# First token block on plain f32 passes, W_out decoded between its products, row sums in two accumulators, and a fixed order at the start

## The chip, the cores and the metric

The kernel runs on one core of one Trainium2 chip. The metric is the device time in microseconds of one execution, as the median of several runs. TensorE is called PE, VectorE DVE, ScalarE ACT, GpSimd POOL; SP is the queue on SyncE that issues all transfers.

## The reference

Agent attention over four batches, and a feed-forward layer on what it gives. q, k and the agents are normal with a spread of 0.8, v with 0.1; the weights are float64.

```python
B, N, C = (4, 12480, 128)       # q, k, v: [4, 12480, 128]; agents: [4, 49, 128]
n_tokens, d_model, d_ff = (49920, 128, 2048)

def sm(a, b):
    s = scale * (a @ b.transpose(0, 2, 1))
    s = s - s.max(-1, keepdims=True)
    e = np.exp(s)
    return e / (e.sum(-1, keepdims=True) + 1e-09)
a2k = sm(agents, k)
agent_v = a2k @ v
q2a = sm(q, agents)
x = (q2a @ agent_v).reshape(B * S, D)
h = x @ w_in
g = h - np.tanh(h)
return (g @ w_out).astype(np.float32)
```

## The kernel before

**Two parts.** For each batch a first phase makes `avs`, the normalized agent_v turned to [128 channels, 49 agents] and written twice side by side, and multiplies it by W_in. The result, 98 rows of 2048 hidden units, is stored as a rounded part `awh` (the type that TensorE takes in one pass) and the rest `awl`. The main part then runs over 104 blocks of 480 tokens, 26 a batch. A block has eight steps `i`; a step handles two chunks of 128 hidden units:

- `m1` (L441, L442): four products, `awh` and `awl` with the block's transposed softmax weights `pT`, into the PSUM tile `h` (three buffers).
- `act`: y = tanh on ACT (L451), z = y squared on ACT (L453), g = h z on DVE (L455).
- `high` (L485): POOL rounds g to `gh`. `low` (L490): DVE takes the rest, `gl`. They run one step behind.
- `m2` (L502 to L504): per chunk three products, `wo_l` with gh, `wo_h` with gh, `wo_h` with gl, summed in a PSUM tile of the pool `misc` (two buffers). The last step of every even block is "plain": one f32 product a chunk with the unrounded copy `wo_f` (L500), and neither gh nor gl.

The softmax of q (`q_softmax`, two blocks at a time: L396, L406 to L421) and its transposes (`q_transpose`, L428, L433) run beside this, and so do the first phases of batches 1 to 3 (generators in `kq`, three started in each pair of blocks).

**The start.** Batch 0 has no block to hide behind. Its first phase reads K in 13 tiles of up to 1024 keys (`kt`), forms the scores (L212), copies them to `s` (ACT, L223) and takes maxima (DVE, L225). After the last tile the maxima are joined and spread as `mb` (L267). Then per tile of V: subtract (DVE, L276), exponential (ACT, L278), product with V (L292). The row sums are formed by adding all tiles of exponentials in `es` (DVE, L305), a reduction (L308) and three products with a column of ones (L316). `sums` adds the two halves of the PSUM tile, divides, transposes (L338) and writes `avs` (L340, L343). `project` makes awh and awl in five parts (L370, L373, L374), and takes the maximum of each part (L376) for a test that comes at the very end.

**The weights.** W_in and W_out come as raw 64-bit words in pieces of 512 columns (`raw`). `decode` turns a piece to f32: one operation on ACT (L128) and six on DVE (L129 to L134). For W_out, `load_w_out` then makes `wo_h` (ACT, L156), `wo_l` (DVE, L157) and from the last piece `wo_f` (ACT, L159). Two pieces of W_out are loaded among the K tiles and decoded during the V stage, two come behind the V tiles and are decoded behind `avs`.

**What sets the order.** Each engine runs its instructions in the order of the built program. A scheduler that simulates a timeline chooses it; `hold` adds the few edges that keep some decode work on DVE behind a named instruction, and `loads_first` keeps the early transfers in the order written.

Of the kernel before, what the change touches and what calls it, by code (L numbers as in the profile page):

```python
# [15 lines left out]
I64 = mybir.dt.int64  # L16
# [33 lines left out]
R0 = 6  # L50
# [6 lines left out]
NB = dict(y=2, z=2, g=4, gh=3, gl=2)  # L57
QL = 0
# [17 lines left out]
class Build:  # L76
# [19 lines left out]
    def constants(self):  # L96
# [7 lines left out]
        nc.vector.tensor_copy(self.identr, self.ident)  # L104
        self.ones = c.tile([128, 128], F32, tag="ones", name="ones")
# [8 lines left out]
        for vt in self.vb:  # L114
            nc.gpsimd.memset(vt[:, :, C : C + 1], 1.0)
# [3 lines left out]
    def decode(self, raw, dst):  # L119
# [8 lines left out]
        nc.scalar.activation(size, hi.bitcast(F32), AF.Abs)  # L128
        nc.vector.tensor_scalar(ta, hi, 3, 0x3FFFFFF8, ALU.logical_shift_left, ALU.bitwise_and)  # L129
        nc.vector.scalar_tensor_tensor(ta, hi, 0xC0000000, ta, ALU.bitwise_and, ALU.bitwise_or)  # L130
# [3 lines left out]
        nc.vector.scalar_tensor_tensor(dst, size, TINY, rem, ALU.is_ge, ALU.mult)  # L134
# [605 lines left out]
```

## Time and profile before

| what | value |
|---|---|
| median of 3 runs | 2185.13 us (2184.85 to 2185.13) |
| the profiled execution | 2180.92 us, its span 2179.1 us |
| busy in the span | PE 98%, DVE 93%, ACT 83%, POOL 64% |
| chain that ended last | PE 88%, DVE 6%, POOL 3%, waiting to issue 2% |
| batch 0's last K product | starts at 30.0 us |
| first and last product with V | 35.1 and 50.5 us |
| `avs` complete | 59.6 us |
| first tanh, first g of block 0 | 70.3 and 73.0 us |

The profiled execution is 4.2 us shorter than the median, 0.2%. Times inside it are us from the start of the span. A product of f32 operands appears as two records, one of the rounded type as one. A group's mean is the time of one instruction; followers on one engine overlap a little, so the distance between two starts can be shorter.

### The profile page before, as it was taken

The page shows a single profiled execution, that of the slowest core. Times are in us where ns is not written, and L with a number is a line of the kernel's source. Part 1 is how long each engine was busy: PE and PEld are TensorE (multiplying, and loading weights), DVE is VectorE, ACT ScalarE, POOL GpSimd, SP SyncE. Part 2 cuts the span into 40 slices and gives each one's busy share as a digit, 9 for nine tenths or more (in the row PEclk, how much of TensorE's full clock was granted, in tenths as well). Part 3 has the DMA queues.
Part 4 walks back from the last instruction along what each step waited for, and adds up shares of the span by engine and source line. Part 5 has one row for each costly group of instructions (what it writes and reads, how often), then busy time and mean ns, then how long its engine had stood idle before and what let it go on. Part 6 is the DMA issues. An engine that isn't in the chain of part 4 may idle for free.

```text
span 2179.1 us, 31204 instructions
## 1 busy us (share of the span) xinstructions
PE 2144.5 (98%) x11089; PEld 1799.3 (83%) x11089; DVE 2026.2 (93%) x2120; ACT 1813.1 (83%) x2179; POOL 1395.5 (64%) x933
## 2 busy tenths in 40 slices
PE   7899999999999999999999999999999999999998
PEld 7688878888888887888888888888888888888887
DVE  7898999999999999889999999998999999999998
ACT  4688888888888788888898878888889898989987
POOL 1356567666666556667666556667667677676766
PEclk9799999999999999999999999999999999999999
DMA  9211111110011111111101110121100101010000
GB/s 353 86 58 60 56 38 57 59 57 28 28 48 57 59 48 46 58 59 48 37 19 57 57 50 19 56 65 33 36 20 19 37 19 37 19 37 19 28 10 20
DMA packets 65906, 108.75 MB, mean 50 GB/s; under 512 B 4048, under 2 KB 44240, under 8 KB 65744
## 3 DMA queue, kind: packets, MB, share of 16 engines
q1 hardware_dynamic: 65744, 106.68, 15.2%
q8 instruction: 91, 1.49, 0.3%
q14 instruction: 71, 0.58, 0.1%
HBM read 81.10 MB, written 25.56 MB: 49 GB/s over the span
## 4 chain that ended last, share of the span: by engine, by line
PE 88%; DVE 6%; POOL 3%; issue 2%; ACT 0%; DMA 0%; POOLq 0%; SPq 0%; DVEq 0%; ACTq 0%
PE h L441 15%; PE h L442 15%; PE misc L504 15%; PE misc L502 14%; PE misc L503 14%; PE misc L500 4%; PE misc L396 4%; PE misc L238 3%; POOL gh L485 2%; DVE gl L490 2%; DVE g L455 2%; PE misc L292 2%; PE misc L428 1%; PE h L212 1%; PE misc L370 0%
## 5 line engine op out<-in xcount | busy, mean ns | idle before, releaser
L485 POOL TENSOR_SCALAR gh<-g 128x960 fp32r<-128x960 f32 x780 | 1207.3, 1549 | 665.0 <-DVE g L455 416.5
L490 DVE TENSOR_TENSOR gl<-g,gh 128x960 fp32r<-128x960 f32 x780 | 977.4, 1254 | 89.8 <-PE misc L504 55.7
L455 DVE TENSOR_TENSOR g<-h,z 128x960 f32<-128x960 f32 x832 | 950.5, 1146 | 30.5 <-ACT z L453 27.3
L451 ACT ACTIVATE y<-h 128x960 f32<-128x960 f32 x832 | 802.9, 970 | 186.2 <-PE h L442 182.1
L453 ACT ACTIVATE z<-y 128x960 f32<-128x960 f32 x832 | 832.4, 1007 | 24.3 <-DVE g L455 7.2
L441 PE MATMUL h<-pT,awh 98*128 98x480 f32 x1664 | 662.0, 398 | 1.9 <-DVE awl L374 1.4
L442 PE MATMUL h<-pT,awl 98*128 98x480 f32 x1664 | 631.7, 380 | 0.3 <-DVE awl L374 0.3
L504 PE MATMUL misc<-gl,wo_h 128*128 128x480 f32 x1560 | 607.6, 390 | 3.0 <-DVE gl L490 2.9
L502 PE MATMUL misc<-gh,wo_l 128*128 128x480 f32 x1560 | 601.8, 386 | 4.9 <-POOL gh L485 4.9
L503 PE MATMUL misc<-gh,wo_h 128*128 128x480 f32 x1560 | 593.9, 381 | 0.0
L441 PEld LDWEIGHTS h<-pT,awh 98*128 98x128 f32 x1664 | 313.5, 188 | 65.9 <-issue 13.2
L442 PEld LDWEIGHTS h<-pT,awl 98*128 98x128 f32 x1664 | 315.2, 189 | 57.5 <-issue 10.5
L502 PEld LDWEIGHTS misc<-gh,wo_l 128*128 128x128 f32 x1560 | 294.4, 189 | 59.9 <-POOL gh L485 15.7
L504 PEld LDWEIGHTS misc<-gl,wo_h 128*128 128x128 f32 x1560 | 292.6, 188 | 56.4 <-DVE gl L490 7.9
L503 PEld LDWEIGHTS misc<-gh,wo_h 128*128 128x128 f32 x1560 | 293.3, 188 | 47.1 <-issue 1.2
L409 POOL TENSOR_TENSOR qe<-qe,qm 120x392 f32<-120x392 f32 x52 | 74.2, 1426 | 63.7 <-ACT qe L407 63.7
L396 PEld LDWEIGHTS misc<-ag,qt 128*120 128x120 f32 x832 | 96.3, 186 | 4.0 <-issue 0.3
L617 ACT ACTIVATE o<-misc 128x480 f32<-128x480 f32 x104 | 58.7, 564 | 48.7 <-PE misc L500 33.6
L396 PE MATMUL misc<-ag,qt 128*120 128x49 f32 x832 | 93.6, 265 | 0.0
L500 PE MATMUL misc<-g,wo_f 128*128 128x480 f32 x208 | 92.9, 569 | 0.0
L421 POOL TENSOR_TENSOR pp<-qe,pp 120x392 fp32r<-120x392 f32 x52 | 69.4, 1335 | 36.6 <-ACT pp L419 36.4
L238 PEld LDWEIGHTS misc<-ag,kt 128*128 128x128 f32 x588 | 72.1, 191 | 2.5
(92 smaller groups left out, 864.0 us busy)
## 6 DMA issues: line engine op xcount, KB each, us to landing
qt<-qT SPq DMA_DIRECT2D x52, 480.0 KB, 3.4
outT<-o SPq DMA_DIRECT2D x52, 480.0 KB, 2.6
kt<-kT SPq DMA_DIRECT2D x48, 512.0 KB, 3.6
v<-v SPq DMA_DIRECT2D x36, 512.0 KB, 4.1
vt<-v SPq DMA_DIRECT2D x12, 512.0 KB, 9.4
raw<-w_in SPq DMA_DIRECT2D x4, 512.0 KB, 9.1
raw<-w_out SPq DMA_DIRECT2D x4, 512.0 KB, 8.9
kt<-kT SPq DMA_DIRECT2D x4, 128.0 KB, 2.1
```

What stands on the lines that cost most here:

```text
L396: nc.tensor.matmul(ps[:TT, t * A : (t + 1) * A], qt[:, t * TT : (t + 1) * TT], self.ag[:, b, :], start=True, stop=True)
L441: nc.tensor.matmul(h[:, c, :BLK], aw[0][:A2, sl], pT[:A2], start=True, stop=False)
L442: nc.tensor.matmul(h[:, c, :BLK], aw[1][:A2, sl], pT[:A2], start=False, stop=True)
L451: nc.scalar.activation(y, h[:, :, :BLK], AF.Tanh, scale=TSC)
L453: nc.scalar.activation(z, y.rearrange("p c n -> p (c n)"), AF.Square)
L455: nc.vector.tensor_tensor(self.pair(g), h[:, :, :BLK], self.pair(z), ALU.mult)
L485: self.nc.gpsimd.tensor_scalar(gh, g, 1.0, 0.0, ALU.mult, ALU.add)
L490: self.nc.vector.tensor_tensor(gl, g, gh.bitcast(F32), ALU.subtract)
L500: nc.tensor.matmul(acc[:, :BLK], self.wo_f[:, c, :], gh[:, x], start=first, stop=last)
L502: nc.tensor.matmul(acc[:, :BLK], self.wo_l[:, f, :], gh[:, x], start=first, stop=False)
L503: nc.tensor.matmul(acc[:, :BLK], self.wo_h[:, f, :], gh[:, x], start=False, stop=False)
L504: nc.tensor.matmul(acc[:, :BLK], self.wo_h[:, f, :], gl[:, x], start=False, stop=last)
```

## The change

**Block 0 in f32.** Every step of block 0 is plain: its products take W_out in f32 (`wf`, 2048 columns, kept in the buffer that batch 1's `awh` will take) and the unrounded g. So block 0 needs no gh, no gl and neither half of W_out. **Decode between its products.** `decode` becomes a generator; its steps are taken by hand, three at a time, before and between the steps of block 0, in work tiles that gh and gl do not use yet. All four pieces of W_out load behind V, into the four buffers that batch 1's V takes later (the ones in their last column are set after). `split_w_out` makes wo_h on ACT and wo_l now on POOL, one piece at each of four steps of block 1. **Row sums.** Two accumulators `es` take turns and are joined; a product with a matrix of ones spreads the sums to all 128 rows. **Sums by selection.** One product of the PSUM halves with `sel` (two stacked 49-column identities) adds the halves and transposes; one DVE operation divides and writes both copies of avs. **Late maxima.** The five maxima of batch 0 move to block 3. **Order.** From the first maxima to the end of block 0, DVE and ACT are held to the written order, and PE in block 0. The q products of the first pair stand ahead of V's products, those of the second pair beside the sums.

```diff
-R0 = 6
+R0 = 4
+LATE = 3
+Q0 = 2
+NV = 10
+SPLIT = (8, 9, 11, 13)
...
     def raw_w_out(self, c):
-        return self.raw(self.wo.rearrange("(n p) e -> p n e", p=128)[:, 4 * c : 4 * c + 4, :])
+        raw = self.vb[c].rearrange("p t c -> p (t c)")[:, :1024]
+        src = self.wo.rearrange("(n p) e -> p n e", p=128)[:, 4 * c : 4 * c + 4, :]
+        self.nc.sync.dma_start(raw.bitcast(I64).rearrange("p (n e) -> p n e", e=C), src)
+        return raw
...
     def load_w_out(self, c, raw):
-        nc = self.nc
-        w = self.work.tile([128, 512], F32, tag="wf", name="wf", bufs=1)
-        self.decode(raw, w)
+        one, two = self.wtile("gl", NB["gl"]), self.wtile("gh", NB["gh"])
+        cut = lambda t, k: t[:, 512 * k : 512 * (k + 1)]
+        return self.decode(raw, self.wf[:, c * 512 : (c + 1) * 512], cut(one, 0), cut(one, 1), cut(two, 0), cut(two, 1))
+
+    def split_w_out(self, c):
...
         nc.scalar.copy(h, w)
-        nc.vector.tensor_tensor(l, w, h.bitcast(F32), ALU.subtract)
+        nc.gpsimd.tensor_tensor(l, w, h.bitcast(F32), ALU.subtract)
+        nc.gpsimd.memset(self.vb[c][:, :, C : C + 1], 1.0)
...
+                if g in (0, 1):
+                    return
+                if g in (2, 3):
+                    st["es", g % 2] = self.small.tile([128, GT * A], F32, tag="ke", name="es")
+                es = st["es", g % 2]
+                e0 = st["s"][:, (g - 2) * GT * A : (g - 1) * GT * A] if g in (2, 3) else es
+                nc.vector.tensor_tensor(es, e0, flat, ALU.add)
                 if g == NG - 2:
+                    es = st["es", 0]
+                    nc.vector.tensor_tensor(es, es, st["es", 1], ALU.add)
...
+                nc.vector.tensor_copy(an[:n, :C], st["ps"][:n, :C])
+                pt = self.misc()
+                nc.tensor.matmul(pt[:, :A], an[:n, :C], self.sel[:n], start=True, stop=True)
+                sm = self.small.tile([128, A], F32, tag="mb", name="mb")
+                nc.vector.tensor_scalar(sm, st["pr"], EPS, None, ALU.add)
+                nc.vector.reciprocal(sm, sm)
+                yield
+                two = [128, 2, A]
+                nc.vector.tensor_tensor(
+                    self.avs[:, b, :].rearrange("p (two a) -> p two a", a=A),
...
             for g in range(NG):
-                if g == 4:
-                    loads.append((q0, 0))
                 loads.append((self.v0, g))
-            loads += [(load_raw, 6), (load_raw, 7)]
+            loads += [(load_raw, 4), (q1_load, 1)] + [(load_raw, c) for c in (5, 6, 7)]
...
+        q1 = q_job(1)
+        next(q1)
+        for _ in range(3):
+            next(sums)
+        next(q1)
+        go(dec[0], 3)
+        run(sums)
+        next(q1)
+        run(rest0.pop(0))
+        go(dec[0], 1)
+        run(rest0.pop(0))
+        run(dec[0])
...
-            plain = even and i == PLAIN_PAIR
+            plain = n == 0 or even and i == PLAIN_PAIR
...
+            if n == LATE and i < NP:
+                first = self.count()
+                self.bound(0, i, slice(PCUT[i], PCUT[i + 1]))
+                self.hold(first, mark)
...
+            if n == 0:
+                if i == 0:
+                    run(rest0.pop(0))
+                if i % 2 == 0 and i < HP - 2:
+                    go(dec[i // 2 + 1], 3)
+                elif i < HP - 2:
+                    run(dec[i // 2 + 1])
+            if pos in SPLIT and n < 2:
+                first = self.count()
+                self.split_w_out(SPLIT.index(pos))
+                self.hold(first, mark, (ET.Activation, ET.Pool))
             out(LAG2)
+            if n == 0 and i == HP - 1:
+                self.issue_order(ET.DVE, at)
+                self.issue_order(ET.Activation, at)
+                self.issue_order(ET.PE, early)
...
-            if (pos + 2) % 16 in KS and kq and n % NBLK < 25:
+            if (pos + 2) % 16 in KS and kq and 0 < n and n % NBLK < 25:
                 start(kq.pop(0))
```

**Where instructions stand.** On DVE, from avs to the first g of block 0. Before (`raw`, `da`, `db`, `rem`, `wf` are the decode's tiles, `mx` the maxima):

```order
L340 COPY avs<-misc 128x49
L129 TENSOR_SCALAR da<-raw 128x512 x2
L130 SCALAR_TENSOR_TENSOR da<-raw,da 128x512 x2
L131 TENSOR_SCALAR db<-da 128x512
L374 TENSOR_TENSOR awl<-h,awh 98x256
L376 TENSOR_REDUCE mx<-awh 49x1
L131 TENSOR_SCALAR db<-da 128x512
L132 SCALAR_TENSOR_TENSOR rem<-raw,db 128x512 x2
L133 TENSOR_TENSOR rem<-da,rem 128x512 x2
L374 TENSOR_TENSOR awl<-h,awh 98x512
L134 SCALAR_TENSOR_TENSOR wf<-de,rem 128x512
```

After (the decode's work tiles are `gh` and `gl`, its raw words stand in `v_90` and so on, its result `wf` in the buffer of batch 1's `awh`, whose name it bears here):

```order
L137 TENSOR_SCALAR gh<-v_90 128x512
L139 SCALAR_TENSOR_TENSOR gh<-v_90,gh 128x512
L141 TENSOR_SCALAR gh<-gh 128x512
L362 TENSOR_TENSOR avs<-misc,mb 128x98
L448 TENSOR_REDUCE qm<-misc 120x8
L413 TENSOR_TENSOR awl<-h,awh 98x256
L143 SCALAR_TENSOR_TENSOR gl<-v_90,gh 128x512
L413 TENSOR_TENSOR awl<-h,awh 98x512
L145 TENSOR_TENSOR gl<-gh,gl 128x512
L147 SCALAR_TENSOR_TENSOR awh<-gl 128x512
L497 TENSOR_TENSOR g<-h,z 128x960
L413 TENSOR_TENSOR awl<-misc,awh 98x512
```

Before, the decode of two pieces, with their split, stands between avs and the first g. Now half of one piece stands ahead of avs and the other half behind it, and the first g comes seven places after avs.

On PE in block 0, from the fourth part of W_in's product on. After (L542 are the f32 products, L483 and L484 `m1`):

```order
L409 MATMUL misc<-w_in,avs 98x512
L542 MATMUL misc<-g,awh 128x480 x2
L483 MATMUL h<-pT,awh 128x480
L484 MATMUL h<-pT,awl 128x480
L483 MATMUL h<-pT,awh 128x480
L484 MATMUL h<-pT,awl 128x480
L542 MATMUL misc<-g,awh 128x480 x2
L483 MATMUL h<-pT,awh 128x480
L484 MATMUL h<-pT,awl 128x480
```

Before, from the same part on (L396 are q's products):

```order
L370 MATMUL h<-w_in,avs 98x512
L502 MATMUL misc<-gh,wo_l 128x480
L503 MATMUL misc<-gh,wo_h 128x480
L396 MATMUL misc<-ag,qt 120x49
L441 MATMUL h<-pT,awh 128x480
L442 MATMUL h<-pT,awl 128x480
L441 MATMUL h<-pT,awh 128x480
L442 MATMUL h<-pT,awl 128x480
L396 MATMUL misc<-ag,qt 120x49 x6
L504 MATMUL misc<-gl,wo_h 128x480
L502 MATMUL misc<-gh,wo_l 128x480
```

The three rounded products a chunk have become one f32 product a chunk (two a step), `m1` of one step stands between the pairs, and the second q products have moved ahead, beside the sums.

On POOL at the start of block 1. Before, from the first work after the constants:

```order
L409 TENSOR_TENSOR qe<-qe,qm 120x392
L421 TENSOR_TENSOR pp<-qe,pp 120x8x49
L485 TENSOR_SCALAR gh<-g 128x960 x4
L409 TENSOR_TENSOR qe<-qe,qm 120x392
L485 TENSOR_SCALAR gh<-g 128x960
L421 TENSOR_TENSOR pp<-qe,pp 120x8x49
L485 TENSOR_SCALAR gh<-g 128x960 x16
```

After:

```order
L451 TENSOR_TENSOR qe<-qe,qm 120x392
L463 TENSOR_TENSOR pp<-qe,pp 120x8x49
L451 TENSOR_TENSOR qe<-qe,qm 120x392
L177 MEMSET v_90 128x8
L176 TENSOR_TENSOR wo_l<-awh,wo_h 128x512
L463 TENSOR_TENSOR pp<-qe,pp 120x8x49
L527 TENSOR_SCALAR gh<-g 128x960
L177 MEMSET v_91 128x8
L527 TENSOR_SCALAR gh<-g 128x960
L176 TENSOR_TENSOR wo_l<-awh,wo_h 128x512
L527 TENSOR_SCALAR gh<-g 128x960
L177 MEMSET v_92 128x8
```

The four gh of block 0's first steps are gone; ones for batch 1's V and the subtractions that give `wo_l` stand between the first gh of block 1.

More of the change, by code (lines that the diff above doesn't have):

```diff
@@ L67, in run, with go @@
         pass
+def go(job, steps):
+    for _ in range(steps):
+        next(job, None)
 def run_value(make, *args):
@@ L104, in constants @@
         nc.vector.tensor_copy(self.identr, self.ident)
+        self.sel = c.tile([128, A], F32, tag="sel", name="sel")
+        for r in (slice(0, HALF), slice(HALF, 128)):
+            nc.vector.tensor_copy(self.sel[r], self.ident[r, r.start : r.start + A])
         self.ones = c.tile([128, 128], F32, tag="ones", name="ones")
@@ L147, in load_w_in @@
     def load_w_in(self, c, raw):
-        self.decode(raw, self.w_in[:, c * 512 : (c + 1) * 512])
+        tiles = (self.work.tile([128, 512], F32, tag=t, name=t, bufs=2) for t in ("de", "rem", "da", "db"))
+        run(self.decode(raw, self.w_in[:, c * 512 : (c + 1) * 512], *tiles))
     def load_w_out(self, c, raw):
+        one, two = self.wtile("gl", NB["gl"]), self.wtile("gh", NB["gh"])
+        cut = lambda t, k: t[:, 512 * k : 512 * (k + 1)]
+        return self.decode(raw, self.wf[:, c * 512 : (c + 1) * 512], cut(one, 0), cut(one, 1), cut(two, 0), cut(two, 1))
@@ L270, in av @@
         def av(g):
[L271 removed]
+            vt = ahead("v", load_v, g, vb - 1) if b else None
             n = tiles(g)
@@ L499, in m2 @@
             if gl is None:
-                nc.tensor.matmul(acc[:, :BLK], self.wo_f[:, c, :], gh[:, x], start=first, stop=last)
+                nc.tensor.matmul(acc[:, :BLK], wf[:, c * C : (c + 1) * C], gh[:, x], start=first, stop=last)
                 continue
@@ L507, in last_name, with hold, issue_order, last_on @@
         return self.nc.cur_bb.bb.instructions[-1].name
-    def hold(self, first, name):
+    def hold(self, first, name, engines=(ET.DVE,)):
         info = mybir.DependencyInfo(mybir.DependencyClass.NoSync, mybir.DependencyReason.DATA)
         for i in list(self.nc.cur_bb.bb.instructions)[first:]:
-            if i.engine == ET.DVE:
+            if i.engine in engines:
                 self.tc.add_manual_dep(i, name, info, reason="order on VectorE")
+    def issue_order(self, engine, first):
+        info = mybir.DependencyInfo(mybir.DependencyClass.NoSync, mybir.DependencyReason.DATA)
+        last = None
+        for i in list(self.nc.cur_bb.bb.instructions)[first:]:
+            if i.engine == engine:
+                if last is not None:
+                    self.tc.add_manual_dep(i, last, info, reason="issue order")
+                last = i.name
+    def last_on(self, engine):
+        return next(i.name for i in reversed(self.nc.cur_bb.bb.instructions) if i.engine == engine)
+    def count(self):
+        return len(self.nc.cur_bb.bb.instructions)
     def loads_first(self, early):
```

159 lines of the change are left out of this document (90 added, 69 removed).

## The prediction

> **What bounds the kernel now.** I read the page first (busy shares), then the stretches of 5 us at the start, then the engines in order of time from 28 to 100 us.
>
> ```profile
> span 2179.1 us, 31204 instructions
> PE 2144.5 (98%) x11089; PEld 1799.3 (83%) x11089; DVE 2026.2 (93%) x2120; ACT 1813.1 (83%) x2179; POOL 1395.5 (64%) x933
> ```
>
> ```profile
> 50.00:55.00 5.00, 1.20 (x12) 0.64 (x8) 4.97 (x9) 2.72 (x5) 1.25 (x1) 0.89 1.10 361
> 55.00:60.00 5.00, 1.90 (x12) 1.60 (x13) 3.49 (x12) 0.43 (x2) 0.00 (x0) 0.50 1.06 266
> 60.00:65.00 5.00, 4.54 (x9) 2.12 (x8) 5.00 (x12) 1.29 (x3) 0.00 (x0) 0.50 0.07 10
> 65.00:70.00 5.00, 3.68 (x7) 1.40 (x5) 3.59 (x7) 1.65 (x4) 0.00 (x0) 0.50 0.83 309
> 70.00:75.00 5.00, 2.72 (x5) 1.56 (x6) 3.43 (x5) 4.97 (x8) 0.72 (x1) 0.50 0.00 1
> 75.00:80.00 5.00, 5.00 (x24) 3.87 (x23) 4.74 (x6) 2.77 (x4) 4.09 (x3) 0.72 0.02 3
> 80.00:85.00 5.00, 5.00 (x26) 4.28 (x25) 4.12 (x6) 2.63 (x5) 1.23 (x2) 1.00 0.11 18
> ```
>
> The columns after the stretch are busy us (and instructions) of PE, PEld, DVE, ACT and POOL, then PEclk, the DMA share and GB/s. PE is busy 98% of the span. Where it falls short is here: 1.20 to 1.90 us of 5 in the two stretches from 50, and from 55 to 75 the granted clock is 0.50. From 80 on PE is full at clock 1.00 and stays so. A microsecond by which PE enters that state earlier is therefore a microsecond off the end, and a microsecond of PE work added there is one on it. The change rewrites 30 to 90 us; the rest moves by what that gains.
>
> I measure both kernels at one mark: PE's first product of block 1 (the 33rd of L441/L442, after four for each of block 0's eight steps).
>
> ```profile
> 91.70 0.38 PE L441 MATMUL h<-pT,awh 98*128 98x480 f32 x1
> ...
> 93.44 1.88 PE L238 MATMUL misc<-ag,kt 128*128 128x49 f32 x16
> ...
> 98.75 1.77 PE L500 MATMUL misc<-g,wo_f 128*128 128x480 f32 x4
> ...
> 100.58 0.38 PE L442 MATMUL h<-pT,awl 98*128 98x480 f32 x1
> 100.80 0.38 PE L441 MATMUL h<-pT,awh 98*128 98x480 f32 x1
> ```
>
> In the kernel before the mark is at 91.70. Two prices come from the same rows. Passes of a rounded product follow each other at 0.22 us (100.58, 100.80). The four records of the two plain f32 products begin at 98.75, and the product behind them must have begun 0.22 before 100.58, at 100.36: 1.61 us for a pair, where six rounded passes take 6 x 0.218 = 1.31.
>
> **The change part by part.** First the way to avs (the agents' normalized sums).
>
> ```profile
> 28.89 0.68 ACT L128 ACTIVATE de<-raw 128x512 f32<-128x512 f32 x1 [0.24 <-DMA raw<-w_out]
> ...
> 33.12 0.21 DVE L267 COPY mb<-misc 128x49 f32<-128x49 f32 x1 [0.51 <-PE misc L264]
> 35.09 4.10 PE L292 MATMUL h<-vt,s 128*64 128x128 f32 x36 [2.01 <-ACT s L278]
> 39.12 2.38 PE L396 MATMUL misc<-ag,qt 128*120 128x49 f32 x16
> 41.44 9.29 PE L292 MATMUL h<-vt,s 128*64 128x128 f32 x160
> ...
> 42.16 0.56 DVE L406 TENSOR_REDUCE qm<-misc 120x8 f32<-120x392 f32 x1
> ...
> 51.27 1.25 POOL L421 TENSOR_TENSOR pp<-qe,pp 120x392 fp32r<-120x392 f32 x1 [4.49 <-ACT pp L419]
> ...
> 51.64 1.44 DVE L134 SCALAR_TENSOR_TENSOR wf<-de,rem 128x512 f32<-128x512 f32 x1
> ...
> 55.87 0.81 DVE L308 TENSOR_REDUCE es<-es 128x49 f32<-128x392 f32 x1
> ...
> 59.44 0.20 ACT L343 COPY avs<-misc 128x49 f32<-128x49 f32 x1 [4.70 <-DVE avs L340]
> ```
>
> ```profile
> L455 DVE TENSOR_TENSOR g<-h,z 128x960 f32<-128x960 f32 x14 | 15.8, 1151 | 2.2 <-ACT z L453 2.2
> ...
> L305 DVE TENSOR_TENSOR es<-es,s 128x392 f32<-128x392 f32 x10 | 5.6, 559 | 0.1
> ...
> L130 DVE SCALAR_TENSOR_TENSOR da<-raw,da 128x512 uint32<-128x512 uint32 x8 | 5.4, 687 | 0.1
> ...
> L129 DVE TENSOR_SCALAR da<-raw 128x512 uint32<-128x512 uint32 x8 | 3.2, 421 | 6.4 <-DMA raw<-w_in 6.4
> ```
>
> The second fence groups the operations of the first 110 us by shape: busy us, then mean ns. Followers overlap by about 0.07 us, so a 392-wide step costs 0.49.
>
> K stage. W_out's first two pieces leave the queue ahead of the last K tiles, and ScalarE no longer stops for them (28.89: 0.68 us, after 0.24 us of waiting for the transfer). Bounds 0 (PE sets the pace anyway) and 0.9; I take 0.7, by the operation itself: mb at 32.6 instead of 33.3.
>
> V stage. PE idled 2.0 us before 35.09, for the first exponentials, and at 39.12 put 2.38 us of q products between V products. Now these stand first, in that gap. Then V's 36 records at half clock (4.10) and 160 at full (9.29): 32.7 + 2.4 + 4.1 + 9.3 = 48.5. With the early start the clock should open earlier too (0.114 us a record until 39, 0.058 from 41); 15 of the 36 records at the lower price give 0.8 back, and the eight transposes that now stand before the last V tiles cost about 0.5. They wait for pp: from qm (42.16) to pp's end (52.52) it took 10.4 us, of which DVE's decode held some 2; from 35.2 that is 43.6 to 45.6, when PE reaches them anyway. V's end: 48.2.
>
> Row sums. VectorE had to put 8.6 us of decode (two pieces, 2 x 0.42 and 5 x 0.69 each) between the adds and came out at 56.68, six us after V's last product. Now it has 13 subtractions and 11 adds at 0.49 (11.8), the q softmax (three 392-wide passes and two small ones, 2.1), the reduction (0.81) and a wait of 1.3 for the q products: 32.8 + 16.0 = 48.8, about 49. Two accumulators only take the wait between adds away, and one extra add pays for it: 0. So the sums start at 48.9, not at 56.7.
>
> From there to avs before: 59.64 - 56.68 = 2.96. After: three products with ones, a copy of 113 rows, the selection product behind four q products, and on VectorE three decode steps (0.42 + 0.69 + 0.42) between the reciprocal and avs. About 3.0 again, bounds 2.3 (the q products run at full clock) and 4.5. The new waits sit here. The first decode step waits for W_out's first piece and the q products for q's second load, both issued behind the last V tile, with avs queued behind each.
>
> ```profile
> vt<-v SPq DMA_DIRECT2D x12, 512.0 KB, 9.4
> raw<-w_out SPq DMA_DIRECT2D x4, 512.0 KB, 8.9
> ```
>
> Issued at about 41, they land at 50 by the 8.9 us of a full queue, and about 3.5 sooner once it drains: 0 to 1.1, within the bounds. avs at 51.9: **gain 59.64 - 51.9 = 7.7**.
>
> Second, avs to the first g.
>
> ```profile
> 60.90 0.37 ACT L373 CAST awh<-h 98x256 fp32r<-98x256 f32 x1 [0.57 <-PE h L370]
> ...
> 69.97 0.41 ACT L159 COPY wo_f<-wf 128x256 f32<-128x256 f32 x1
> 70.28 1.83 ACT L451 ACTIVATE y<-h 128x960 f32<-128x960 f32 x2
> ...
> 73.04 2.22 DVE L455 TENSOR_TENSOR g<-h,z 128x960 f32<-128x960 f32 x2 [1.57 <-ACT z L453]
> ```
>
> Before: ScalarE could not start tanh until 70.28, because W_out's casts and the copy of wo_f (69.97) stood ahead of it and waited for VectorE's decode; the first of the two g ended at about 74.1, 14.5 us after avs. After, those casts are gone from here. What remains is awh at 1.6 after avs (59.64 to 61.27 before), awl 0.4, two products at half clock 0.8, y and z 1.0 each (two y take 1.83 above), g 1.15, and handoffs 0.8: 6.75. VectorE's own row (two awl, three decode steps) ends at about 4.9, before z. **Gain 14.5 - 6.7 = 7.8**; bounds 6.5 (another second for the q softmax's copy that stands ahead of awh on ScalarE) and 8.5.
>
> Third, first g to the mark. Before: 91.70 - 74.1 = 17.6. After, VectorE leads: five more g (5.75), three awl (1.8), nine first-half decode steps (4.6) and six second-half ones (4.1), 16.25; then the pair of f32 products of that g, 1.6. PE needs in this time five such pairs (8.0), five groups of four products (4.4) and 0.5 for the last projection, 12.9 at full clock, so it waits for VectorE. That is where the f32 passes cost nothing more (seven pairs x 0.30 = 2.1 us of PE work lie in VectorE's shadow), and where the decode is not hidden: without it PE would lead. If the clock is still half at the start, 0 to 3.4; I take 0.5. **Loss 18.3 - 17.6 = 0.7**.
>
> Fourth, what PE still owes at the mark. Before: products of steps 5, 6, 7 (1.31 + 1.31 + 1.61 = 4.2). After: two f32 pairs (3.2) and one K-scores job of batch 1 that now starts later (1.7, row 93.44). **Loss 0.7**.
>
> Fifth, block 1. GpSimd now makes wo_l: four subtractions of 128x512, with no such row before.
>
> ```profile
> L485 POOL TENSOR_SCALAR gh<-g x20: 994/1446/1998, 83.2 to 138.4; 128x960 fp32r<-128x960 f32 x20
> L421 POOL TENSOR_TENSOR pp<-qe,pp x52: 944/1226/1923, 51.3 to 2119.5; 120x392 fp32r<-120x392 f32 x52
> L409 POOL TENSOR_TENSOR qe<-qe,qm x52: 839/1382/3459, 43.3 to 2110.9; 120x392 f32<-120x392 f32 x52
> ```
>
> By elements from its two-input rows (392): 1.23 at the best (944), 1.6 to 1.8 at the medians, 4.5 at the worst (3459). At 1.8 four of them with five gh (1.45) and the pp product (1.23) are 15.7 us in the five steps in which PE needs 5 x 2.17 = 10.9 plus the transposes; some of it starts during block 0's last products. I take a **loss of 1.5**, bounds 0 and 8. A block lasts 2179 / 104 = 21 us; by the page's shares ScalarE idles 17% of it, 3.5 us, which holds its part of the split (four casts and a copy, 2.9), and VectorE 7%, 1.5. The five maxima moved to block 3 cost VectorE about as much as five 512-wide steps at the most (2.8 to 3.4), twice its slack there: **loss 0.4**, bounds 0 and 2.8. The memsets, the selection matrix and the five W_out and q transfers elsewhere cost nothing: VectorE and GpSimd idle at the start and the DMA share was 0.07 from 60 to 65. V of batch 1 loads later, since its buffers hold W_out, but is wanted ten blocks later.
>
> Sum: 7.7 + 7.8 - 0.7 - 0.7 - 1.5 - 0.4 = 12.2 us. The profiled execution took 2180.92 (span 2179.1 and 1.8 around it); the median of the runs is 2185.13, 4.2 more, which I take as the same for both. 2185.1 - 12.2 = **2172.9**.
>
> **The rivals.** (a) GpSimd becomes the bound of block 1. For: VectorE's step at 51.64 took 1.44 instead of 0.69 just while GpSimd's subtraction ran (51.27 to 52.52), and GpSimd's slowest of that kind took 3.46; so the two hold each other up. Against: gh has a median of 1.45 in a steady state full of gl. At 4.5 each, four subtractions cost 4 x 2.7 = 10.8 more, of which some 8 less the 1.5 already counted reach PE: 2172.9 + 6.5 = 2179.4. The Trainium skill, page "SBUF — State Buffer", section "SBUF: two separate sides", says that the two engines share a port pair as an exclusive lock, against VectorE operations with two SBUF inputs. By that rule the subtraction waits out each gl and each gl waits for it: the sum would end at this rival's 2179; the two rows agree with it, but g reads PSUM, so the lock leaves gaps.
>
> (b) Slower: the clock stays half. For: from 60 to 70 PE was busy 4.54 and 3.68 of 5 and the clock did not open; it opened only after 75 to 80 was full. If PE keeps getting gaps from VectorE, every us at half clock in which PE leads costs half a us; PE has 16.25 - 12.9 = 3.3 to spare in block 0. Half clock from 53 to 95 would cost 21 - 3.3 = 17.7 and end at 2172.9 + 17.7 = 2190.6; it turns into a loss when the clock opens later than about 84 (31 x 0.5 - 3.3 = 12.2). Against: at half clock PE needs 2 x (0.87 + 1.61) = 5.0 us a step, VectorE 16.25 / 5 = 3.3, so PE would have no gaps, and a full PE opened the clock above. The Trainium skill, page "TensorE: Matmul & The Clock Gate", Part 1, gives a free-running window of 3.4 us that must be busy; by that the clock opens within two windows of full work, at a cost of up to 3.4, and the sum would end at 2172.4 to 2175.8; the row of 75 to 80 agrees.
>
> (c) V sets its own pace: tiles 8 to 11 are requested only when V's first are used, at 36.9 and on, and land 9.4 later (row above): V ends at 50 to 51. Gain 10 to 11, 2174 to 2175. Against: the queue is shorter by then.
>
> (d) No change: (a) and a late W_out together, 2181 to 2187.
>
> **Chances.** Forecast, 2168 to 2177 with (c) inside it: 0.70 (of that (c) 0.12); better than 2168, if sums start with V's end and the clock opens early: 0.09; (a), 2177 to 2181: 0.12; (d) 0.05; (b) 0.04. Faster by over 0.2% (4.4 us, about what a measurement here can tell from none), below 2180.7: 0.70 + 0.09 + 0.12 = 0.91; within it 0.05; slower 0.04. Range 2165 to 2181.
>
> **What would show it.** Right: the reduction of es ends near 48.9 and avs near 52; tanh starts within 4 us of avs; VectorE has no gap over 1 us between the first and sixth g; the mark is at 76 to 78; PE waits under 2 us for gh in block 1. Wrong: PEclk 0.50 beyond 65; GpSimd's wo_l above 3 us; avs behind a wait for W_out; PE gaps at block 3.

## The result, and the profile after

The changed kernel takes 2172.63 us (median of 6 runs, 2170.77 to 2173.20), the kernel before, run beside it, 2185.13 (2182.78 to 2186.27): a ratio of 0.9943, 95% interval 0.9930 to 0.9955, 12.5 us less. The forecast was 2172.9. The profiled execution of the changed kernel took 2170.77, the lowest of its six, with a span of 2168.9; that of the kernel before 2180.92. So the two profiles differ by 10.2 us and the medians by 12.5; what follows explains the 10.2 first.

The head of the page, and the stretches of 5 us at the start of the changed kernel (busy us of PE, PEld, DVE, ACT, POOL, then PEclk, DMA share, GB/s):

```profile
span 2168.9 us, 31164 instructions
PE 2142.6 (99%) x11076; PEld 1792.2 (83%) x11076; DVE 2018.4 (93%) x2109; ACT 1813.3 (84%) x2178; POOL 1389.1 (64%) x930
```

```profile
50.00:55.00 5.00, 4.40 (x29) 3.34 (x28) 3.25 (x10) 0.78 (x3) 0.57 (x1) 1.00 1.07 382
55.00:60.00 5.00, 4.57 (x17) 2.70 (x16) 4.57 (x8) 4.44 (x6) 0.39 (x2) 1.00 1.02 368
60.00:65.00 5.00, 5.00 (x16) 2.81 (x16) 4.86 (x8) 4.90 (x8) 0.00 (x0) 1.00 0.16 43
...
85.00:90.00 5.00, 3.92 (x22) 3.16 (x21) 4.11 (x4) 4.48 (x6) 2.83 (x3) 1.00 0.00 0
...
105.00:110.00 5.00, 4.46 (x24) 3.52 (x22) 5.00 (x6) 4.16 (x6) 4.22 (x3) 1.00 0.17 69
```

From 50 to 60 PE was busy 3.1 us of 10 before; now 9.0, at clock 1.00 instead of 0.50 to 0.89. New are the holes behind 85, in block 1, where PE had been full. The engines in order of time (start, length, what it waited for in brackets):

```profile
32.76 2.30 PE L438 MATMUL misc<-ag,qt 128*120 128x49 f32 x16
...
35.10 0.56 DVE L448 TENSOR_REDUCE qm<-misc 120x8 f32<-120x392 f32 x1 [0.94 <-PE misc L438]
...
44.11 4.17 DVE L334 TENSOR_TENSOR es<-es,s 128x392 f32<-128x392 f32 x7
48.31 0.57 DVE L337 TENSOR_TENSOR es<-es 128x392 f32<-128x392 f32 x1
48.91 0.82 DVE L339 TENSOR_REDUCE es<-es 128x49 f32<-128x392 f32 x1
...
53.11 0.25 DVE L362 TENSOR_TENSOR avs<-misc,mb 128x98 f32<-128x98 f32 x1
...
56.09 0.97 ACT L493 ACTIVATE y<-h 128x960 f32<-128x960 f32 x1 [0.53 <-PE h L484]
...
58.14 1.16 DVE L497 TENSOR_TENSOR g<-h,z 128x960 f32<-128x960 f32 x1 [0.39 <-ACT z L495]
...
73.68 1.15 DVE L497 TENSOR_TENSOR g<-h,z 128x960 f32<-128x960 f32 x1
...
76.81 0.38 PE L484 MATMUL h<-pT,awl 98*128 98x480 f32 x1
```

The row sums end at 49.73 (56.68 before), avs at 53.36 (59.64), the first g at 59.30 (74.19); the sixth g ends at 74.83, and the mark is 0.22 ahead of 76.81, at 76.6 (91.70). So the kernel enters its steady state 15.1 us earlier. Block 1 then:

```profile
85.87 1.29 POOL L176 TENSOR_TENSOR wo_l<-awh,wo_h 128x512 fp32r<-128x512 f32 x1
...
92.35 1.29 POOL L176 TENSOR_TENSOR wo_l<-awh,wo_h 128x512 fp32r<-128x512 f32 x1
```

```profile
83.90 1.15 DVE L532 TENSOR_TENSOR gl<-g,gh 128x960 fp32r<-128x960 f32 x1
85.94 2.24 DVE L532 TENSOR_TENSOR gl<-g,gh 128x960 fp32r<-128x960 f32 x1 [0.89 <-POOL gh L527]
...
92.50 2.15 DVE L532 TENSOR_TENSOR gl<-g,gh 128x960 fp32r<-128x960 f32 x1
```

```profile
88.23 0.48 PE L546 MATMUL misc<-gl,wo_h 128*128 128x480 f32 x1 [1.08 <-DVE gl L532]
...
103.11 0.49 PE L546 MATMUL misc<-gl,wo_h 128*128 128x480 f32 x1 [0.28 <-DVE gl L532]
...
106.10 0.48 PE L544 MATMUL misc<-gh,wo_l 128*128 128x480 f32 x1 [0.54 <-POOL gh L527]
```

A gl that begins 0.1 us behind a wo_l subtraction ends 1.0 us behind that subtraction's end (87.16 and 88.18; 93.64 and 94.65) and takes 2.2 us instead of 1.15. PE waits for it.

How much of the 15.1 is left is read from the copies of the blocks' outputs. First the kernel before (blocks 1, 2 and 25), then the changed one (blocks 2 and 25; block 1's ends at 108.28):

```profile
121.63 0.57 ACT L617 ACTIVATE o<-misc 128x480 f32<-128x480 f32 x1 [0.20 <-PE misc L504]
...
141.88 0.57 ACT L617 ACTIVATE o<-misc 128x480 f32<-128x480 f32 x1 [0.33 <-PE misc L500]
...
615.53 0.55 ACT L617 ACTIVATE o<-misc 128x480 f32<-128x480 f32 x1
```

```profile
127.99 0.58 ACT L698 ACTIVATE o<-misc 128x480 f32<-128x480 f32 x1
...
605.28 0.55 ACT L698 ACTIVATE o<-misc 128x480 f32<-128x480 f32 x1
```

The lead is 13.8 to 13.9 us at the outputs of blocks 1 to 6 and 12 to 18 (in between the two kernels have jobs at different places) and 10.25 at block 25. The step down is no new loss: the changed kernel starts batch 1's jobs in block 1 instead of block 0 and stays two jobs behind, at block 1's end two K jobs of 1.7 us, 3.4 us of PE work, at blocks 12 to 18 two of the jobs with V. It does them when the kernel before has run out of such jobs (the lead falls by 3.5 from block 18 to 25). The true lead behind block 1 is thus 13.9 - 3.4 = 10.5, and it stays: 10.25 at block 25, 9.9 at block 103, 10.2 in the span.

| step of the prediction | forecast | the two profiles |
|---|---|---|
| K stage, V stage, row sums, avs | 7.7 | 59.64 - 53.36 = 6.3 |
| avs to the first g | 7.8 | 14.5 - 5.94 = 8.6 |
| first g to the mark | -0.7 | 17.5 - 17.3 = +0.2 |
| owed at the mark | -0.7 | -0.7 (as counted: two f32 pairs, one K job) |
| block 1 | -1.5 | 10.5 - (15.1 - 0.7) = -3.9 |
| maxima in block 3 | -0.4 | 0.0 (lead 13.88 behind block 2, 13.85 behind 3) |
| sum | 12.2 | 10.5 |

### The profile page after: what moved, and what is told of

It is laid out like the page before. It is cut to its first block, busy times and chain, and to the rows that moved or that the text cites. A ratio compares the mean times of both kernels' runs of the same rounds, so it can differ in the third digit from the quotient of the medians.

```text
span 2168.9 us, 31164 instructions
## 1 busy us (share of the span) xinstructions
PE 2142.6 (99%) x11076; PEld 1792.2 (83%) x11076; DVE 2018.4 (93%) x2109; ACT 1813.3 (84%) x2178; POOL 1389.1 (64%) x930
## 3 DMA queue, kind: packets, MB, share of 16 engines
q1 hardware_dynamic: 65744, 106.68, 15.1%
## 4 chain that ended last, share of the span: by engine, by line
PE 88%; DVE 6%; POOL 3%; issue 2%; ACT 1%; DMA 0%; POOLq 0%; SPq 0%; DVEq 0%; ACTq 0%
PE h L483 15%; PE h L484 15%; PE misc L546 15%; PE misc L544 14%; PE misc L545 14%; PE misc L542 4%; PE misc L438 4%; PE misc L258 3%; POOL gh L527 3%; DVE g L497 2%; DVE gl L532 2%; PE misc L314 2%; PE misc L470 1%; PE h L232 1%; ACT z L495 0%
## 5 line engine op out<-in xcount | busy, mean ns | idle before, releaser
L497 DVE TENSOR_TENSOR g<-h,z 128x960 f32<-128x960 f32 x832 | 951.0, 1147 | 32.6 <-ACT z L495 29.0
L483 PE MATMUL h<-pT,awh 98*128 98x480 f32 x1664 | 664.2, 399 | 0.0
L484 PE MATMUL h<-pT,awl 98*128 98x480 f32 x1664 | 632.4, 380 | 0.0
L544 PE MATMUL misc<-gh,wo_l 128*128 128x480 f32 x1546 | 594.1, 384 | 5.3 <-POOL gh L527 4.9
L545 PE MATMUL misc<-gh,wo_h 128*128 128x480 f32 x1546 | 587.8, 380 | 0.0
L483 PEld LDWEIGHTS h<-pT,awh 98*128 98x128 f32 x1664 | 312.5, 188 | 63.8 <-issue 14.1
L484 PEld LDWEIGHTS h<-pT,awl 98*128 98x128 f32 x1664 | 314.1, 189 | 59.0 <-issue 12.7
L542 PE MATMUL misc<-g,wo_f 128*128 128x480 f32 x204 | 91.1, 569 | 0.0
```

The source lines that it names most:

```text
L483: nc.tensor.matmul(h[:, c, :BLK], aw[0][:A2, sl], pT[:A2], start=True, stop=False)
L484: nc.tensor.matmul(h[:, c, :BLK], aw[1][:A2, sl], pT[:A2], start=False, stop=True)
L497: nc.vector.tensor_tensor(self.pair(g), h[:, :, :BLK], self.pair(z), ALU.mult)
L542: nc.tensor.matmul(acc[:, :BLK], wf[:, c * C : (c + 1) * C], gh[:, x], start=first, stop=last)
L544: nc.tensor.matmul(acc[:, :BLK], self.wo_l[:, f, :], gh[:, x], start=first, stop=False)
L545: nc.tensor.matmul(acc[:, :BLK], self.wo_h[:, f, :], gh[:, x], start=False, stop=False)
```

## The experiments

Each kernel is the changed one with the edit shown. Totals are medians; the changed kernel has 2172.63. It and seven of the twelve have the same instructions on VectorE and PE up to the end of the row sums, and these eight executions still reach it between 49.66 and 52.08 us. So stages are compared within an execution: from the end of es to that of avs, from there to the first g's end, from there to the sixth.

**Decode first.** The generator steps between the products of block 0 are dropped and all pieces run ahead of it.

```diff
-        run(dec[0])
+        for d in dec:
+            run(d)
...
-                if i % 2 == 0 and i < HP - 2:
-                    go(dec[i // 2 + 1], 3)
-                elif i < HP - 2:
-                    run(dec[i // 2 + 1])
```

> All four pieces of W_out are decoded ahead of block 0's first step; no decode stands between its products. Theory (the prediction's): 9.6 us of decode (three more pieces of 3.2 us on VectorE) then stand between avs and the first g, 15 us after avs instead of 5.94, as in the kernel before (14.5); from the first g to the sixth PE leads with about 13 us instead of 15.5; the mark comes about 7 us later, the total is 6 to 9 us above the changed kernel. Rival: VectorE does the same sum of work in either order and makes it up by the mark: total within 1.5 us of the changed kernel.

2184.22 (ratio to the kernel before 1.0003, 0.9993 to 1.0012): the whole gain is gone, 11.6 us, more than the 6 to 9 expected.

```profile
53.57 2.84 PE L409 MATMUL h<-w_in,avs 128*98 128x256 f32 x4
...
72.13 3.47 PE L542 MATMUL misc<-g,awh 128*128 128x480 f32 x4 [10.45 <-DVE awl L413]
```

es (49.66) and avs (53.28) stand as in the changed kernel; the first g ends at 71.47, 18.2 us behind avs. PE waits 10.45 us for VectorE, and the granted clock is 0.50 for 10.2 us from 65.1, which I had not counted. That the row sums end 7 us earlier is worth nothing while the decode follows them in one lump.

**No fixed order.**

```diff
-                self.issue_order(ET.DVE, at)
-                self.issue_order(ET.Activation, at)
-                self.issue_order(ET.PE, early)
```

> The fixed issue order on VectorE, ScalarE (from the end of K) and PE (block 0) is left out; the compiler's scheduler chooses. In its order nearly all decode steps of W_out's four pieces stand ahead of the first g on VectorE, and the q softmax's steps behind more row-sum adds. Theory: the gain hangs on the order, not on the new instructions: the first g comes 8 to 11 us later than 5.94 us after avs, PE idles meanwhile and its clock falls, and the total is 8 to 12 us above the changed kernel, like the kernel with all decode first (2184.2). Rival: the scheduler's order does the same work in the same time, VectorE being the bound either way: total within 1.5 us.

2183.10 (0.9994, 0.9984 to 1.0003). The scheduler puts decode steps ahead of avs too, where they wait for W_out:

```profile
47.29 0.85 DVE L339 TENSOR_REDUCE es<-es 128x49 f32<-128x392 f32 x1
...
50.30 0.43 DVE L137 TENSOR_SCALAR gh<-v 128x512 uint32<-128x512 uint32 x1 [1.69 <-DMA v<-w_out]
53.08 0.43 DVE L137 TENSOR_SCALAR gh<-v 128x512 uint32<-128x512 uint32 x1 [2.35 <-DMA v<-w_out]
...
59.47 0.25 DVE L362 TENSOR_TENSOR avs<-misc,mb 128x98 f32<-128x98 f32 x1
...
69.53 1.15 DVE L497 TENSOR_TENSOR g<-h,z 128x960 f32<-128x960 f32 x1
```

es ends at 48.14, avs 11.6 us behind it (3.6 in the changed kernel), the first g 11.0 behind avs. The size was as expected, the way half different: the wait that the prediction had named as a possible cost of the first decode step (W_out's landing) is what VectorE runs into here.

**Decode between the adds again**, for two of the four pieces, loaded among the K tiles:

```diff
             for g in range(5, NG):
                 run(av[g])
+                if g in (5, 9):
+                    c = (g - 5) // 4
...
+                    run(self.decode(raws[4 + c], self.wf[:, c * 512 : (c + 1) * 512], *tiles))
```

> Undoes one part: W_out's first two pieces are loaded among the K tiles and decoded between the row-sum adds again, behind the 6th and the 10th V group; the last two stay in block 0. Theory: VectorE's decode between the adds (2 x 3.6 us) was what held the row sums; the reduction of es ends near 57 instead of 49.73, avs near 59.5. Block 0 then has 6.4 us less decode on VectorE, so that PE leads it (12.9 instead of 15.5 us from the first to the sixth g at least): the mark is 3 to 5 us later than 76.6 and the total 3 to 5 us above the changed kernel. Rival: the row sums came earlier because V's products did (q products moved ahead, clock open sooner), not because of the decode: es ends at 51 at the latest, and with less decode in block 0 the total is 0 to 2 us below the changed kernel.

2179.60 (0.9981, 0.9972 to 0.9991), 7.0 above the changed kernel, not 3 to 5.

```profile
57.13 0.66 PE L326 MATMUL h<-es,ones 128*128 128x49 f32 x2 [6.28 <-DVE es L339]
```

V's products were done, and PE waited 6.28 us for es, which ended at 57.07: the decode held the sums, and the rival falls. What block 0 got back (13.4 us from the first g to the sixth instead of 15.5) was lost to a clock of 0.50 from 55.4 to 65.6: from avs to the first g it took 8.8 us instead of 5.9.

**One piece decoded**, used for all of block 0:

```diff
-        dec = [self.load_w_out(c, raws[4 + c]) for c in range(4)]
+        dec = [self.load_w_out(c, raws[4 + c]) for c in range(1)]
```

> Only W_out's first piece is decoded, and all of block 0 and the splits use it, so three quarters of W_out's values are wrong and 9.6 us of VectorE's work in block 0 are left out. Theory: decode makes VectorE lead block 0 (15.53 us from the first g to the sixth): without it PE leads with about 13 us, the mark is 2 to 3 us nearer to the first g and the total 2 to 3.5 us below the changed kernel. Rival: PE's f32 passes and ScalarE take as long anyway: mark and total change by less than 0.5 us.

From the first g to the sixth 12.0 us (59.95 to 71.99, starts) instead of 15.5: VectorE does lead block 0 through the decode, by 3.5 us. The lead at the output of blocks 0 to 10, less the later start of this execution (es 1.8 later), is 2.5 us, as expected; in the median (2171.79) 0.8 is left, within the spread of single runs.

**First decode steps behind avs.**

```diff
-        go(dec[0], 3)
         run(sums)
...
-        go(dec[0], 1)
+        go(dec[0], 4)
```

> The first three decode steps of W_out's first piece (0.36 + 0.69 + 0.43 us on VectorE in the changed kernel) move from between the reciprocal and avs to behind the first projection. Theory: they hold avs, whose selection product is done at 51.98 while avs ends at 53.36; avs then ends near 52.3, 1.1 earlier. Behind avs they stand in the same VectorE row in which 0.83 us was idle before awl, so the first g (end 59.30) and the mark (76.6) come 0.4 to 0.9 earlier, and the whole kernel is 0.4 to 0.9 us faster than the changed one. Rival: PE's q products, which end at about 52.8, and ScalarE's copy of them, which stands ahead of awh, set the time anyway: the first g stays at 59.3, total 0.

2172.54. avs ends 2.54 us behind es instead of 3.63, the 1.1 expected; but the first g ends 7.78 behind avs instead of 5.94, so it is 0.75 later than before. The steps do hold avs, but behind it VectorE has no idle time left between the first awl and the first g, so that they cost more there: the place ahead of avs is the cheaper one.

**No wo_l in block 1.**

```diff
-        nc.gpsimd.tensor_tensor(l, w, h.bitcast(F32), ALU.subtract)
```

> GpSimd's four wo_l subtractions (1.28 us each) are left out of block 1; wo_l is filled with zeros in the K stage, so the low parts of W_out's weights do not enter the result. Theory: the subtractions cost block 1 most of what it lost (PE waits of 2.7 us between the mark and block 1's output, the largest, 1.08, on a gl that took 2.24 instead of 1.15 us while a subtraction ran): PE's waits there fall under 1 us, every gl takes 1.15, block 1's output copy ends 2 to 3 us earlier than 108.28, and the total is 2 to 3 us below the changed kernel. Rival: ScalarE's casts and copy of the split (2.9 us) hold y and z up: waits stay above 2 us, total 0 to -0.7.

2171.37. Against block 0's output the outputs of blocks 2 to 6 come 2.4 us earlier than in the changed kernel (block 1's own 3.4 earlier, of which block 2 loses 1.0 again), and PE has no wait left there. So the subtractions are 2.4 of block 1's 3.9. The other 1.5 stays open; the ScalarE part of the split was not tried alone.

```profile
86.64 1.15 DVE L533 TENSOR_TENSOR gl<-g,gh 128x960 fp32r<-128x960 f32 x1
88.69 1.16 DVE L533 TENSOR_TENSOR gl<-g,gh 128x960 fp32r<-128x960 f32 x1 [0.90 <-POOL gh L528]
```

**The split in block 0.**

```diff
-SPLIT = (8, 9, 11, 13)
+SPLIT = (1, 3, 5, 7)
```

> The four splits of W_out (ScalarE's cast, GpSimd's wo_l subtraction) are issued in block 0, behind steps 1, 3, 5 and 7, where GpSimd is idle, instead of block 1. Theory: a subtraction of GpSimd and a VectorE operation with two operands in SBUF exclude each other (in four traces a gl that began 0.1 us behind a wo_l ended 1.0 us behind it and took 2.15 to 2.25 instead of 1.15 us). In block 0 VectorE leads and its decode steps read SBUF, so each subtraction holds it by up to 1.28: from the first g to the sixth 16.5 to 18 us instead of 15.53; block 1 gets 2.4 us back; total -1 to +2 us against the changed kernel. Rival: block 1 lost because GpSimd had too much to do there, without exclusion: the stretch stays at 15.5 and the total falls by 2 to 2.5.

2173.26. From the first g to the sixth 17.4 us, and block 1 gets 2.85 back (2.6 from block 4 on). This decides between exclusion and load:

```profile
69.19 1.79 POOL L176 TENSOR_TENSOR wo_l<-awh,wo_h 128x512 fp32r<-128x512 f32 x1 [3.35 <-DMA v<-v]
```

```profile
69.15 0.69 DVE L139 SCALAR_TENSOR_TENSOR gh<-v,gh 128x512 uint32<-128x512 uint32 x1
69.88 1.39 DVE L141 TENSOR_SCALAR gh<-gh 128x512 uint32<-128x512 uint32 x1
71.19 1.15 DVE L497 TENSOR_TENSOR g<-h,z 128x960 f32<-128x960 f32 x1
```

The subtraction begins inside L139 and takes 0.5 longer, the rest of L139; L141 begins inside the subtraction (to 70.98) and ends 0.3 behind it, 1.39 instead of 0.43. Two more decode steps lost time beside a subtraction, 1.08 instead of 0.68 and 0.97 instead of 0.41; with L141 that is 1.9 us, all that the stretch grew by. A g, which reads PSUM, kept its 1.15 beside another subtraction (63.53, beside 63.83 to 65.12). The Trainium skill, page "SBUF — State Buffer", section "SBUF: two separate sides", says that the one that starts first holds the shared port pair for its whole instruction and the other blocks. The rows here agree, on both sides.

**f32 passes into block 1.**

```diff
-            plain = n == 0 or even and i == PLAIN_PAIR
+            plain = n == 0 or n == 1 and i < 4 or even and i == PLAIN_PAIR
...
-SPLIT = (8, 9, 11, 13)
+SPLIT = (12, 14, 8, 10)
```

> Steps 0 to 3 of block 1 use f32 passes with the decoded W_out too, so four gh (GpSimd) and four gl (VectorE) fall away there, and the four splits are issued at positions 8, 10, 12, 14 (third and fourth piece first). Theory: block 1's loss is GpSimd's and VectorE's load; PE does 4 x 0.30 = 1.2 us more, its waits (2.7 us) go: 1 to 2 us faster than the changed kernel. Rival: PE would have made up those waits later anyway, or ScalarE holds block 1: 1.2 us slower.

2172.27. Between the outputs of blocks 0 and 2 it gains 0.8 us on the changed kernel, less than the 1 to 2 expected (waits of 0.42 and 0.43 are left); in the total that cannot be told from nothing.

**The add on GpSimd.**

```diff
-        nc.vector.tensor_tensor(rem, ta.bitcast(F32), rem, ALU.add)
+        eng.tensor_tensor(rem, ta.bitcast(F32), rem, ALU.add)
...
-                    go(dec[i // 2 + 1], 3)
+                    go(dec[i // 2 + 1], 5)
```

> In block 0 the fifth of the six decode steps (an addition, 0.69 us on VectorE) of W_out's last three pieces goes to GpSimd, which is idle there; the first four steps stand between one pair of g, the sixth behind the next. Theory: VectorE leads block 0, GpSimd's addition runs beside g, which reads PSUM, and is not held: from the first g to the sixth 13.5 to 14.2 us instead of 15.53, total 1.3 to 2 us below the changed kernel. Rival: the addition (1.3 us at least) holds the VectorE steps beside it, or arrives late for the sixth step: stretch 15.5 or longer, total 0 to +1.5.

2174.40; from the first g to the sixth 15.7 us, so the theory fails.

```profile
64.17 1.15 DVE L498 TENSOR_TENSOR g<-h,z 128x960 f32<-128x960 f32 x1
65.65 0.69 DVE L148 SCALAR_TENSOR_TENSOR awh<-gl 128x512 f32<-128x512 f32 x1 [0.33 <-POOL gl L146]
```

```profile
64.33 1.28 POOL L146 TENSOR_TENSOR gl<-gh,gl 128x512 f32<-128x512 f32 x1 [8.36 <-DVE gl L144]
```

The addition did run beside g and held nothing, but it ends 0.3 us behind that g, and VectorE waits 0.33 us for it ahead of the sixth step, twice in the stretch: the rival's late addition. These are VectorE's only waits there, so it still leads. And its work has shrunk by one addition only: two are gone, but the fourth step of the last piece has moved in. The steps are uneven now (the g begin 3.9, 2.7, 3.3, 2.4 and 3.3 us apart). The profiled execution, the slowest of its five (2176.07), lost 2.3 us more in block 1, where its clock was at 0.50 for 6.8 us from 92.4.

**The clock.** The last three ask why executions of the same instructions differ. In stretches of 1 us (columns as above), first the changed kernel, then the one with the first decode steps behind avs:

```profile
33.00:34.00 1.00, 1.00 (x12) 1.00 (x11) 0.96 (x3) 0.28 (x1) 0.00 (x0) 1.00 1.01 401
34.00:35.00 1.00, 1.00 (x9) 0.91 (x7) 0.16 (x1) 0.72 (x2) 0.00 (x0) 0.52 1.03 401
...
37.00:38.00 1.00, 1.00 (x18) 1.00 (x16) 1.00 (x2) 0.41 (x2) 0.31 (x1) 0.77 0.17 16
```

```profile
32.00:33.00 1.00, 0.28 (x1) 0.12 (x1) 0.53 (x2) 0.00 (x0) 0.00 (x0) 0.97 1.00 397
33.00:34.00 1.00, 0.62 (x3) 0.53 (x3) 0.29 (x2) 0.00 (x0) 0.00 (x0) 0.50 1.01 406
...
39.00:40.00 1.00, 1.00 (x16) 1.00 (x14) 1.00 (x1) 0.59 (x2) 0.66 (x1) 0.62 0.00 0
```

At two clock values the mean of a stretch tells the part at half clock: 0.96 + 2 + 0.46 = 3.42 us in the first, 0.06 + 6 + 0.76 = 6.82 in the second. Behind PE's gaps around mb the clock falls for one or two such windows. With one, es ends 16.45 to 16.65 us behind mb (three executions), with two 17.08 to 17.79 (five). In four of the eight it falls again between 51 and 55; in the three of them that keep the changed kernel's order the first g then ends 7.0 to 8.1 us behind avs instead of 5.9. The changed kernel's profiled execution had one window and no second fall, which fits its being the lowest of six.

```diff
+            self.nc.tensor.matmul(ps[:, 384:482], self.ident, self.ag[:, 0:2, :], start=True, stop=True)
```

> Adds 22 products whose result nobody reads, into free columns of PSUM: 12 behind the last K product, 5 behind the transposition of the maxima, 5 ahead of avs, to fill PE's gaps there. Theory: those gaps let the granted clock fall to 0.50, for one stretch of 3.2 us (34.0 to 37.2, changed kernel) or two (33.0 to 39.6, 34.5 to 41.3, 33.0 to 39.5 in three other executions with the same start), and again behind 53 in some; that spread is most of the spread between runs. With the gaps filled the clock stays at 1.00 from 30 to 60, the 16 q products take 1.9 us instead of 2.3 to 3.4, es ends at 16.3 us after mb in each execution, and the median is 0.7 to 2 us below the changed kernel's. Rival: the clock falls for another reason than these gaps, and the added products only delay mb: total 0 to 0.5 us slower.

2175.55 (0.9965, 0.9951 to 0.9979). Between 30 and 54 the clock stays at 1.00, and the q products take 1.88 us:

```profile
29.68 2.84 PE L107 MATMUL misc<-ag,ident 128*128 128x98 f32 x24
...
34.73 1.88 PE L449 MATMUL misc<-ag,qt 128*120 128x49 f32 x16
```

es ends 16.23 us behind mb, as expected. But the 12 products make 24 records and take 2.84 us: mb ends at 35.05, 2.0 later than in the changed kernel, and the clock falls at 54.8 all the same.

```diff
-Q0 = 2
+Q0 = 4
```

> The first q tile's softmax stands behind four instead of two V subtractions on VectorE. VectorE idled 0.94 us (2.08 in another execution) for the q products before qm, and from qm to the end of es it took 14.63 us in every execution so far. Theory: two subtractions (0.98 us) fill that gap, es ends 0.9 to 1.0 nearer to mb (16.65 us after it in the changed kernel), total 0.5 to 1 us faster. Rival: pp comes 1 us later, PE's wait for it before the transposes (0.87 us) grows to 1.9, and V's last products set the end of the sums instead: total 0.

2172.55. es ends 16.26 us behind mb in spite of two windows of half clock, as the theory has it, but avs came 4.14 us behind es, and the total is that of the rival: V's last products ended at 49.7, 0.6 behind es, and the products with ones stood behind them. (PE also waited 1.09 us for the second q tile's transfer ahead of the selection product, but that was done at 52.9, when VectorE had just come through the decode steps that stand ahead of avs.)

Both together, with the second q tile loaded earlier:

```diff
+                if g == K0 - 1:
+                    loads.append((q1_load, 1))
...
+                self.warm(ps, 6)
```

> The first try at keeping the clock added too long a row (a product of this kind makes two records, 0.118 us each), which delayed mb by 1.8 us. Now 6 + 2 unread products around the transposition of the maxima, 2 ahead of the products with ones, 2 ahead of avs; one more V subtraction stands ahead of qm; and the second q tile is loaded behind the 8th V tile instead of the last (PE waited 0.21 to 1.09 us for it ahead of the selection product in three traces). Theory: mb stays near 33, the clock stays at 1.00 from 30 on, es ends 15.8 to 16.3 us after mb in every execution, avs 3.6 after es, and the median is 1 to 2 us below the changed kernel's. Rival: the clock falls behind 50 again or PE's wait for pp sets V's end: total within 0.5 us of the changed kernel.

2174.05. es ends 15.77 behind mb, as expected, but now PE waits 0.45 us for one of V's last tiles and does 1.0 us of q products ahead of V's last ones: V's products end at 51.4 and avs stands 5.2 us behind es; the clock fell once, at 36.1. So the theory fails, and not for the rival's reasons: the clock stayed up behind 50, PE did not wait for pp, and the median is 1.4 us above the changed kernel. None of the variants beats the changed kernel beyond the spread of runs.

## Why the prediction was right

- **What bounds the start, and that it is worth its full time: right.** A us by which PE entered its steady state earlier stayed a us to the end (10.5 behind block 1, 10.2 in the span).
- **To avs, 7.7 against 6.3: the size was off.** The row sums ended at 49.7, not 48.9. The K stage gave 0.25 of its 0.7 (mb at 33.08, 32.6 forecast). The wait ahead of qm was 0.94 us (1.3 forecast), but the adds, priced at 0.49 like the subtractions, follow each other at 0.60 (seven from 44.11 to 48.31), which costs 0.9 over eight of them. From es to avs it took 3.6 instead of 3.0, through the three decode steps. That the sums were early because the decode left them is shown by the kernel that puts it back; that V would set its own pace (rival (c)) fell with V's end at 49.2.
- **avs to the first g, 7.8 against 8.6: right**, and the kernels with decode first and without the fixed order show on what it hangs: the order in which VectorE takes decode and g. The prediction had priced the fixed order at nothing, since it costed the order that it makes; without it 10.5 of the 12.5 us are gone. That it took 5.94 us and not the 6.75 forecast is in part luck: the clock was at 1.00 there, while in the three executions named under the clock in which it fell a second time the stretch took 7.0 to 8.1. Tanh began 2.7 us behind avs, within the 4 that were to show it.
- **First g to the mark: right.** VectorE led (15.5 us, forecast 16.25), without decode 12.0 (PE's share was forecast at 12.9).
- **Clock: better than forecast** in this execution. Rival (b) fell: 1.00 from 38 on. But half clock, for which I had put fixed amounts (0.8 less in V's records, 0.5 more in block 0), differs from execution to execution.
- **Block 1, 1.5 against 3.9: the step that failed.** The subtraction was priced at 1.8 us of GpSimd's own time. It takes 1.29, less than that, but the VectorE operation beside it stops for its whole length, and PE waits for that. Rival (a) had this mechanism from the row in which a decode step took 1.44 instead of 0.69, and priced it at 8 us, by subtractions of 4.5 us. They took 1.29 in block 1, only two of the four met a gl there, and leaving them out gives 2.4 back. What the other 1.5 of the 3.9 are stays open.
- **Block 3, 0.4 against 0.0.** The five maxima take 2.8 us together, but they run from 123.1 to 134.2, across the end of block 2, so that the slack of two blocks holds them and not, as I had it, that of one.
- **Profile against median: wrong, and it hid the errors; that the total is only 0.3 us off is luck.** I took the 4.2 us between the profiled execution and the median for both kernels. The changed kernel has 1.9. The 2.3 us so gained make up for the 1.7 that the terms had too much (12.2 against 10.5). The clock is part of the reason why the kernel before lies further from its profile. In 49 more executions of it, timed beside the experiments (one of 5409.62 us is left out), the time on the whole follows the mean granted clock, from 2179.15 us at 0.995 to 2187.83 at 0.990: the 12 at 0.990 take 2185.9 on average, the 14 at 0.992, the value of the profiled execution, 2182.8. The 1.9 us from there to 2180.92 stay open. The six of the changed kernel lie at 0.997 to 0.999, so part of the 12.5 us is probably clock that is no longer lost; no run here separates how much.
- **Not tried alone**: the second accumulator, the selection matrix, the later maxima. The forecast gave the first two no gain, and nothing here contradicts that.

## What to carry to other kernels

When work is moved between the products of a pipeline that it used to precede, the order on the engine that carries both is the change: check what a scheduler would do with the same instructions. Price an operation on GpSimd by what it stops on VectorE, not by its own length, and put it beside operations that read PSUM. And before a profile pair is taken as the difference, see whether the same instructions take the same time in several executions; here one more window at half clock moved a stage by up to 2 us, more than most of the edits tried.

## What the runs showed of the hardware

- **Half clock comes in whole windows.** The stretches at 0.50 in the fourteen profiled executions (without the last stretch of each, which the end of the span cuts off) measure 3.40 to 3.42, 6.82 to 6.84, 10.24 and, in the kernel before, 23.9 us: 1, 2, 3 and 7 times 3.41. The Trainium skill, page "TensorE: Matmul & The Clock Gate", Part 1, section "What's actually happening", gives a free-running window of 3413 ns; the lengths agree, and so does that the phase differs between executions. How much of a window must be idle is open: in one execution gaps of 0.87 us in a window left the clock up (the changed kernel, 44.3 to 47.7), in another 0.56 us, beside products of 49 columns, brought it down (decode first, 48.1 to 51.5).
- **The steady state repeats closely.** Between executions with the same order, offsets mostly stay within 0.1 us over ten blocks and more (0.3 apart at block 7 in some, up to 0.3 adrift by the last block), broken by single steps of 0.8 or 1.1 us, behind block 10 and behind block 33, that some executions have and some have not.
